# A filter stage whose block-diagonal matrix product is run in four 64x64 tiles of TensorE

## The chip, the cores and the metric

The kernel runs on one core of a Trainium2 chip. Its metric is the device time of one execution in microseconds. It was run three times: 1011.85, 1012.19 and 1015.22 us, so the median is 1012.19 us. One more execution was profiled; every duration in this text comes from that one.

Five engines matter: PE (TensorE, the matmuls, with its weight loads shown apart as PEld), DVE (VectorE), ACT (ScalarE), POOL (GpSimd) and SP, which issues most of the DMAs. Each works through its own queue in order. They wait for each other on semaphores.

## The reference, cut to what matters

Two layers alternate, twice: a global spectral filter and a token-mixing MLP, both behind a layer norm and both added to their input. The array has 2048 tokens and 640 channels.

```python
def _A_ref(x, w_r, w_i):
    X = rfft2(x)                  # over tokens and channels
    X = X * (w_r + 1j * w_i)      # 2048 x 321 complex weights
    return irfft2(X, s=(2048, 640))

x = x + _A_ref(layernorm(x), w_r, w_i)
x = x + _B_ref(layernorm(x), ...)     # gelu MLP over the tokens
x = x + _A_ref(layernorm(x), w_r, w_i)
x = x + _B_ref(layernorm(x), ...)
```

The change lies in the middle of A: the last steps of the forward transform, the multiplication by the weights, and the first step of the inverse transform.

## The kernel before, in words

All transforms are products with tables of cosines and sines. To keep nearly float32 precision, a value is split into a high and a low float16 part, and each product is done as three matmuls: high by high, high by low, low by high (`mm3`).

The token axis of 2048 is split as 16 x 128. A first step (`a0_s1`) transforms the 128 part and leaves its result in two SBUF tiles, `s1h` and `s1l`, both `[128, 80, 16, 8]`. The third axis is the group `g` (16 of them), and the last holds 8 numbers: four slots (four frequencies) with a real and an imaginary part each. The method `a1` then works group by group. It runs twice in the kernel, once per filter layer, from 59.9 to 131.7 us and from 564.7 to 634.6 us. These are the steps for a group `g`; the letters are those of the program's order lists:

- `d` (`dstage`, line 495): the channel transform, on PE. Rows of the result are 16 x 8 numbers (16 remainders of the token index by 8 slot parts), and columns are the 321 channel frequencies. There are four classes of channels. Two are cosine classes, whose sums go to PSUM bank 0 (`bk` 0 in `CL`), and two are sine classes, to bank 1. Each has 160 or 161 columns and takes four matmuls: 16 in all. In groups 0 and 1 it takes six per class.
- `ph`, `pl` (`psplit`, line 508): ACT copies the high float16 part of all 642 columns out of PSUM, DVE then makes the low part.
- `s` (`s2stage`, line 531): the transform over the 16 remainders, a 128x128 matrix on PE. For each of two outputs `ri` and two inputs `q` (bank 0 and bank 1 of `d`) there are three matmuls of 321 columns: 12 in all. The matrix mixes only numbers of the same slot.
- `ta`, `tb` (`term`, line 580): DVE multiplies the result in PSUM with the real and with the imaginary weights.
- `sa`, `sb` (`suma`, `sumb`): POOL forms the two sums of the complex product, each over 321 columns.
- `xh`, `uh` and `xl`, `ul`: the split of the product into high and low, `xh` on ACT and `xl` on POOL; `uh` and `ul` are short ACT copies of 63 columns each that repeat a part of them.
- `i` (`is2mm`, line 541): the first inverse step. It has 36 matmuls whose stationary operand has only 64 rows; the two row halves of PE (`q`) alternate.
- `Yh`, `Yl` (`yhi`, `ylo`): ACT copies the high part of the result into the tile `Y`, DVE makes the low part, in two instructions.

The order of all this is written out by hand. `group(g)` (line 647) lists the steps of a group, software-pipelined: in the time of group `g`, PE does `d` of group g+1, `i` of group g-3 and `s` of group g; DVE does `ta`, `tb` of group g-1, `pl` of g+1 and `Yl` of g-3. The loop at line 668 runs the groups 0 to 12, and the list `LAST` (line 24) holds the rest, in which group 15 is cut into two column parts. `Pin` (line 58) keeps each engine in program order. PSUM is four buffers of two banks each (`big`, line 99), taken in turn by `d`, `i` and `s`: a step can begin only when the readers of the buffer taken four steps earlier are done.

Around this, the loop also splits the first weight tile of the next layer into high and low (`wsplit`, lines 672 and 702): a quarter each after groups 8 to 11 on ACT, and in groups 9 to 12 on DVE right behind `pl`. In the first pass some small work on scales is added (`scan1`, `scale1`, `scale_b`) in groups 4 to 8.

Of the kernel before, what the change touches and what calls it, by code (L numbers as in the profile page):

```python
# [12 lines left out]
F16 = mybir.dt.float16  # L13
BF16 = mybir.dt.bfloat16
AF = mybir.ActivationFunctionType
ALU = mybir.AluOpType
# [5 lines left out]
NQ = 8  # L22
NX = 5
LAST = '''
    d14 s13 xh11 uh11 ph14 ta12 tb12 xl11 d15 pl14 s14 ul11 ta13 ph15 i10 tb13 sa12 pl15 sb12 ta14 s15 xh12 sa13 sb13
    tb14 xh13 sa14! uh13 ta15a i11 Yh10 xl12 tb15a xl13 Yl10 uh12 ul12 Yh11 sb14 sa15a s15b xh14 xl14 sb15a! ta15b
    ul13 tb15b i12 sa15b! Yh12 Yl11 uh14 xh15a ul14 i13 Yl12 i14 sb15b xl15a Yh13 xh15b uh15 Yh14 Yl13 xl15b Yl14 i15a
    ul15 Yh15a i15b Yh15b Yl15a Yl15b
# [38 lines left out]
class Layers:  # L67
# [217 lines left out]
    def a0_open(self, first=False):  # L285
        nc, A = self.nc, self.A
        p = self.pS1 = self.push("S1", side=self.sp)
        self.s1h = p.tile([128, 80, 16, 8], F16, name=f"s1h{self.n}")
        self.s1l = p.tile([128, 80, 16, 8], F16, name=f"s1l{self.n}")
        self.tD = p.tile([128, 20, 161], F16, name=f"tD{self.n}")  # L290
        self.tS2 = p.tile([128, 2, 2, 4, 128], F16, name=f"tS2{self.n}")
        self.tI2 = p.tile([128, 2, 2, 2, 128], F16, name=f"tI2{self.n}")
        p = self.pT = self.push("a0", side=self.sp)
        if first:
            self.tM = [p.tile([128, 4, 128], F32, name=f"tM{q}_{self.n}") for q in range(4)]
        else:
            self.tM = [p.tile([128, 4, 2, 128], F16, name=f"tM{q}_{self.n}") for q in range(4)]
# [56 lines left out]
    def a0_s1(self, j, fh, fl):  # L354
        ps = self.big().rearrange("p a b -> p (a b)")
        for t in range(5):
            c = slice(t * 128, t * 128 + 128)
            self.mm3(ps[:, c], (fh[:, c], fl[:, c]), (self.tM[j // 4][:, j % 4, 0], self.tM[j // 4][:, j % 4, 1]), True, True)
        return ps[:, :D].rearrange("p (a b) -> p a b", b=8)

    def a0_s1f(self, j, f):
        ps = self.big().rearrange("p a b -> p (a b)")
        for t in range(5):
            c = slice(t * 128, t * 128 + 128)
            self.PE.matmul(ps[:, c], f[:, c], self.tM[j // 4][:, j % 4], start=True, stop=True)
        return ps[:, :D].rearrange("p (a b) -> p a b", b=8)

    def a0_s1h(self, j, pv, zs=ZS):
        self.T.activation(self.s1h[:, :, j], pv, AF.Copy, scale=S1S / (zs * TS))

    def a0_s1l(self, j, pv, zs=ZS):
        self.V.scalar_tensor_tensor(
            self.s1l[:, :, j], pv, S1S / (zs * TS), self.s1h[:, :, j], op0=ALU.mult, op1=ALU.subtract
        )

    def a0_tail(self, j, z, st, pend):

        V, G, T, p = self.V, self.G, self.T, self.pT
        mv = self.stats2(p, st)
        v = self.t(p, [128, 1], F32, "v", 2)  # L380
        V.tensor_scalar(v, mv[:, 1:2], self.CA, self.CB, op0=ALU.mult, op1=ALU.add)
        m2 = self.t(p, [128, 1], F32, "nm", 2)
        V.tensor_scalar(m2, mv[:, 0:1], 2.0, None, op0=ALU.mult)
        eo = self.t(p, [128, 646], F32, "eo", 2)
        v2 = lambda a, o, w: a[:, o:o + 2 * w].rearrange("p (a b) -> p a b", a=2)[:, :, 0:160]
        za, zb = v2(z, 1, 161), v2(z, 321, 160)
        G.tensor_tensor(v2(eo, 322, 161), za, zb, op=ALU.subtract)
        r = self.t(p, [128, 1], F32, "r", 2)
        G.tensor_tensor(r, v, self.mh, op=ALU.pow)
        V.scalar_tensor_tensor(v2(eo, 1, 161), za, m2, zb, op0=ALU.subtract, op1=ALU.add)  # L390
        V.tensor_scalar(eo[:, 0:162:161], z[:, 0:162:161], mv[:, 0:1], None, op0=ALU.subtract)
        sc = S1S / (ZS * TS)
        m = self.tM[j // 4]
        eb = eo[:, 0:644].rearrange("p (a b) -> p a b", a=2)
        ea, eb = eb[:, :, 0:160], eb[:, :, 161:321]
        fs = []
        for i, (c, w) in enumerate(((slice(0, 128), 512), (slice(128, 160), 128))):
            f = self.t(p, [128, w], F32, f"ft{i}", 1)
            f4 = f.rearrange("p (c b) -> p c b", c=4)
            V.tensor_tensor(f4[:, 0::3], ea[:, :, c], eb[:, :, c], op=ALU.add)  # L400
            V.tensor_tensor(f4[:, 1:3], ea[:, :, c], eb[:, :, c], op=ALU.subtract)
            if i:
                V.tensor_copy(f[:, 95:128:32], eo[:, 160:482:321])
            fh, fl = (self.t(p, [128, w], F16, f"{a}t{i}", 1) for a in ("fh", "fl"))
            T.activation(fh, f, AF.Identity, scale=r)
            fs.append((f, fh, fl))
        ps = []
        for k, f, fh in pend:
            ps.append((k, self.a0_s1(k, *self.a0_lo(f, fh))))
            self.a0_s1h(*ps[-1])  # L410
        qs = []
        for i, (f, fh, fl) in enumerate(fs):
            V.scalar_tensor_tensor(fl, f, r, fh, op0=ALU.mult, op1=ALU.subtract)
            n = f.shape[1]
            q = self.big()[:, 0, :n]
            for o in range(0, n, 128):
                c = slice(o, o + 128)
                self.mm3(q[:, c], (fh[:, c], fl[:, c]), (m[:, j % 4, 0], m[:, j % 4, 1]), True, True)
            qs.append((q.rearrange("p (a b) -> p a b", b=8), slice(64 * i, 64 * i + n // 8)))
        for q in ps:  # L420
            self.a0_s1l(*q)
        for pv, q in qs:
            T.activation(self.s1h[:, q, j], pv, AF.Copy, scale=sc)
            V.scalar_tensor_tensor(
                self.s1l[:, q, j], pv, sc, self.s1h[:, q, j], op0=ALU.mult, op1=ALU.subtract
            )

    def s1_all(self, j, fh, fl):
# [5 lines left out]
    def a1(self, first):  # L434
# [49 lines left out]

        rest = [self.dram.tile([4, 32, NG, 128], F16, name=f"rest{i}_{self.n}") for i in range(2)]
        for q, a in zip(rest, (self.s1h, self.s1l)):
            nc.sync.dma_start(q.rearrange("c i g r -> (c i) g r"), a[:, 64:].rearrange("p g a b -> p g (a b)"))
        stack(G0)

        def wload(g):  # L490
            w = self.t(p, [128, 2, NL], F32, "w", 3)
            nc.sync.dma_start(w, A["w"][g])
            return w

        def dstage(g):
            ps = self.big()
            part = lambda t: tuple(s[:, t * 16 + g].rearrange("p a b -> p (a b)") for s in (self.s1h, self.s1l))
            for c, bk, o0, o1, k in CL:
                out, n = ps[:, bk, o0:o1], o1 - o0
                self.mm3(out, part(c), (self.tD[:, 2 * c, :n], self.tD[:, 2 * c + 1, :n]), True, False)  # L500
                if g < G0:
                    self.mm3(out, part(4), (self.tD[:, 8 + 2 * c, :n], self.tD[:, 9 + 2 * c, :n]), False, True)
                else:
                    i = g % NC
                    mm(out, stk[g - i][:k, c, i], self.tD[:k, 16 + c, :n], start=False, stop=True)
            return ps

        def psplit(ps):
# [17 lines left out]
        def twice(g, i):  # L526

            q = xs[g % NX][i]
            T.activation(q[:, :, NL:], q[:, :, 257:320], AF.Copy)

        def s2stage(g, ph, pl):
            sp = 1 if g == 0 else 0
            ps = self.big()
            for ri in range(2):
                for q in range(2):
                    a = tuple(self.tS2[:, h, sp, 2 * ri + q] for h in range(2))
                    b = (ph[:, q, :NL], pl[:, q, :NL])
                    self.mm3(ps[:, ri, :NL], a, b, q == 0, q == 1)
            return ps

        def is2mm(ps, g, lt):

# [56 lines left out]
        tt = collections.defaultdict(dict)  # L599
        part = {"": every, "a": slice(0, 256), "b": slice(256, NL)}  # L600
        ltile = {"": slice(0, 3), "a": slice(0, 2), "b": slice(2, 3)}
        dst = {}

        def do(op):
            name, g, c, dve = re.fullmatch(r"([a-zY]+)(\d+)([ab]?)(!?)", op).groups()
            g, W = int(g), V if dve else G
            pair = lambda: (tt[g][0], tt[g][1])
            if name == "d":
# [25 lines left out]
            elif name == "xl":  # L634
                xlo(g, part[c], tt[g][0][:, :, part[c]], W)
            elif name in ("uh", "ul"):
                twice(g, name == "ul")
            elif name == "i":
                pv[g, c] = self.big()
                for lt in range(3)[ltile[c]]:  # L640
# [6 lines left out]
        def group(g):  # L647
# [3 lines left out]
                return  # L651
            yield f"d{g + 1}"
            if g > 2:
                yield f"i{g - 3}"
            if g > 1:
                yield f"s{g}"
            if k > 0:
# [1 line left out]
            if k >= 0:  # L659
                yield from (f"ta{k}", f"tb{k}", f"sa{k}", f"sb{k}")  # L660
            yield from (f"ph{g + 1}", f"pl{g + 1}")
            if g > 2:
                yield from (f"Yh{g - 3}", f"Yl{g - 3}")
            if k > 0:
                yield f"ul{k - 1}"

        spare = lambda c: lambda: ps2[max(ps2)][:, 1, c:c + 1]
        for g in range(NG - 3):
# [19 lines left out]
                self.wopen(0)  # L688
            if first and g == 4:
                sb = self.scale_b(at=spare(400))  # L690
            if first and 4 <= g < 8:
                next(sb)
            if first and g in (5, 6):
                self.scan1(0, (g - 5,))
# [1078 lines left out]
def build_tables():  # L1773
# [45 lines left out]
    for sp in range(2):  # L1819
        for c8 in range(8):  # L1820
            slot, ri = c8 // 2, c8 % 2
            r_in = j16 * 8 + c8
            r_out = j16 * 4 + c8 % 4
            for half in range(2):
                m = slot * 32 + half * 16 + k2
# [21 lines left out]
                        i2[sp, 0, m[:, None], ty * 64 + r_out[None]] = pick(fr)  # L1847
                        i2[sp, 1, m[:, None], ty * 64 + r_out[None]] = pick(fi)
                for q, cc in enumerate((ap.real, aq.real, ap.imag, aq.imag)):
                    s2[sp, q, r_in[:, None], m[None]] = cc  # L1850


    d_i = np.zeros((321, 2, 322))
# [120 lines left out]
```

## Time and profile before

| | value |
|---|---|
| profiled execution | 1010.95 us, of which the span from first to last instruction is 1009.1 us |
| runs | 1011.85, 1012.19, 1015.22 us |
| granted TensorE clock | 0.981 on average; 1.00 throughout both passes of `a1` |
| PE busy | 966.7 us (96%), 8235 matmuls |
| DVE busy | 781.1 us (77%) |
| ACT busy | 577.0 us (57%) |
| POOL busy | 297.9 us (30%) |
| first `a1`, 59.88 to 131.65 us | 71.77 us: PE 67.71, DVE 63.06, ACT 48.77, POOL 48.19 busy |
| second `a1`, 564.65 to 634.58 us | 69.93 us: PE 66.29, DVE 61.05, ACT 44.98, POOL 47.71 busy |

Almost every instruction is recorded by one helper, so nearly all rows show line 59; rows are told apart by the names of their tiles. `ps` is a PSUM buffer, `tD`, `tS` and `tI` are the tables of `d`, `s` and `i`. A row such as `ps<-ph,tS 128*128 128x321` is a matmul with a 128x128 stationary operand and 321 columns streamed. The time of a single matmul is its latency, from its start to its last result; in a stream the next begins much earlier, so the spacing of starts is what a matmul costs. The same holds, in a smaller measure, for DVE and ACT.

### The profile page before, as it was taken

What the parts mean: (1) busy time and instruction counts of PE and PEld (TensorE: products, weight loads), DVE (VectorE), ACT (ScalarE), POOL (GpSimd) and SP (SyncE); (2) the same over time, 40 slices, a digit from 0 to 9 for tenths busy, and PEclk for the clock granted to TensorE, in tenths of its full rate; (3) what the DMA queues carried; (4) which work ended last, traced back from release to release, by engine and by line L of the source; (5) the groups of instructions that cost most, each with busy time, mean ns of one, the idle gap of its engine ahead of it and who ended that gap; (6) DMA issues with size and microseconds to landing.
All of it is one profiled execution on the core that took longest, in us unless ns stands there. A gap on an engine that the chain in (4) does not pass through costs nothing.

```text
span 1009.1 us, 20992 instructions
## 1 busy us (share of the span) xinstructions
PE 966.7 (96%) x8235; PEld 720.8 (71%) x8235; DVE 781.1 (77%) x1493; ACT 577.0 (57%) x890; POOL 297.9 (30%) x502
## 2 busy tenths in 40 slices
PE   4889999999999999999999799999999999999998
PEld 3778777667777777777777687776777777677776
DVE  7978978988767885666666699789965567998885
ACT  5857668687666464555543376684734454444531
POOL 6937857512222202222222278574000000000000
PEclk9599999999999999999999999999999999999999
DMA  7865356657667636464431455465544346756411
GB/s 232 278 191 164 117 171 218 223 208 259 216 210 261 240 132 225 126 199 127 126 117 55 146 176 169 131 220 190 168 167 159 136 142 240 243 170 200 146 45 53
DMA packets 67258, 176.44 MB, mean 175 GB/s; under 512 B 7996, under 2 KB 15320, under 8 KB 67160
## 3 DMA queue, kind: packets, MB, share of 16 engines
q1 hardware_dynamic: 59384, 146.92, 45.0%
q0 software_dynamic: 7776, 28.20, 7.5%
q8 instruction: 64, 1.05, 0.4%
q14 instruction: 34, 0.28, 0.1%
HBM read 127.24 MB, written 47.84 MB: 174 GB/s over the span
## 4 chain that ended last, share of the span: by engine, by line
PE 48%; DVE 22%; ACT 12%; POOL 8%; issue 6%; DMA 4%; SPq 0%; ACTq 0%; DVEq 0%; POOLq 0%
PE ps L59 48%; DVE wl L59 3%; POOL eo L59 3%; DVE f L59 3%; DMA xt<-x 2%; DVE st L59 2%; DVE xt L59 2%; ACT junk L59 2%; ACT z L59 2%; ACT wh L59 2%; POOL xt L59 2%; DVE s1l L59 1%; DVE Yl L59 1%; ACT xt L59 1%; DVE hl L59 1%
## 5 line engine op out<-in xcount | busy, mean ns | idle before, releaser
L59 PEld LDWEIGHTS <-wh 128*128 128x128 f16 x2602 | 251.4, 98 | 101.3 <-issue 3.1
L59 PEld LDWEIGHTS <-wl 128*128 128x128 f16 x1610 | 157.5, 98 | 62.2 <-issue 1.0
L59 PE MATMUL ps<-ul,wh 128*128 128x320 f16 x448 | 133.1, 299 | 0.0
L59 PE MATMUL ps<-uh,wl 128*128 128x320 f16 x448 | 133.1, 299 | 0.0
L59 PE MATMUL ps<-uh,wh 128*128 128x320 f16 x416 | 124.3, 299 | 0.0
L59 PE MATMUL ps<-hl,wh 128*128 128x320 f16 x496 | 102.3, 299 | 0.9 <-DVE hl L59 0.9
L59 PEld LDWEIGHTS <-wo 128*128 128x128 f16 x756 | 73.9, 98 | 29.4 <-DVE wo L59 0.8
L59 DVE SCALAR_TENSOR_TENSOR wl<-raw,s,wh 128x896 f16<-128x896 f32 (+2 forms) x64 | 75.1, 1177 | 22.5 <-ACT wh L59 19.6
L59 POOL TENSOR_TENSOR r<-v,mh 128x1 f32<-128x1 f32 x64 | 36.3, 567 | 162.1 <-DVE nm L59 152.6
L59 ACT ACTIVATE junk<-raw 128x896 bf16<-128x896 f32 (+1 forms) x60 | 59.5, 992 | 27.6 <-DMA raw<-w 24.4
L59 PE MATMUL ps<-tDi,Yh 128*128 128x322 f16 x320 | 71.3, 300 | 0.2
L59 ACT ACTIVATE wh<-raw,s 128x896 f16<-128x896 f32 (+2 forms) x68 | 67.1, 1010 | 6.0 <-DVE s L59 5.5
L59 DVE TENSOR_TENSOR f<-eo 128x256 f32<-128x256 f32 (+1 forms) x124 | 39.0, 368 | 40.6 <-POOL eo L59 40.1
L59 POOL TENSOR_TENSOR xt<-xt,ec 128x320 f32<-128x320 f32 x64 | 52.4, 841 | 34.0 <-DVE xt L59 33.9
L59 ACT ACTIVATE z<-xt,nb,r 128x640 f32<-128x640 f32 x31 | 28.5, 919 | 57.0 <-POOL z L59 45.2
L59 PE MATMUL ps<-ph,tS 128*128 128x321 f16 (+2 forms) x288 | 58.5, 286 | 1.3 <-DVE tb L59 1.3
L59 PE MATMUL ps<-u,wo 128*128 128x320 f16 x420 | 59.0, 299 | 0.5 <-DVE wo L59 0.5
L59 DVE BATCH_NORM_STATS2 st<-xt 128x6 f32<-128x320 f32 x126 | 55.3, 481 | 5.2 <-DMA xt<-x 4.5
L59 PE MATMUL ps<-hha,wh 128*128 128x320 f16 x288 | 58.1, 299 | 0.9 <-DVE wh L59 0.9
L59 POOL TENSOR_TENSOR eo<-z 128x320 f32<-128x320 f32 x62 | 53.3, 880 | 17.1 <-ACT z L59 15.1
L59 PE MATMUL ps<-tM,f 128*128 128x128 f32 x160 | 39.5, 426 | 19.6 <-DVE f L59 19.6
L59 PE MATMUL ps<-tDi,Yl 128*128 128x322 f16 x192 | 55.7, 299 | 1.5 <-DVE Yl L59 1.5
(251 smaller groups left out, 2375.9 us busy)
## 6 DMA issues: line engine op xcount, KB each, us to landing
xt<-x SPq DMA_DIRECT2D x79, 320.0 KB
raw<-w SPq DMA_DIRECT2D x32, 512.0 KB
w<-w SPq DMA_DIRECT2D x48, 321.0 KB
x<-xt SPq DMA_DIRECT2D x47, 320.0 KB
raw<-w SPq DMA_DIRECT2D x32, 448.0 KB
raw<-w2z SPq DMA_DIRECT2D x32, 448.0 KB
w1S<-sp POOLq DMA_DIRECT2D x20, 512.0 KB, 3.7
out<-xt SPq DMA_DIRECT2D x15, 320.0 KB
```

Of the source, the lines that this page charges most:

```text
L59: i = f(*a, **k)
```

## The change: four tiles, swapped halves, another order

1. **Layout.** `s1h` and `s1l` become `[128, 80, 2, 16, 4]`: the 8 slot parts are cut into two halves of two slots each, and the half is now the outer index. The 128 rows of `d`'s result are then 64 rows of slots 0 and 1 and 64 rows of slots 2 and 3, and the matrix of `s` becomes two blocks of 64x64. The writers of these tiles (`a0_s1h`, `a0_s1l`, `a0_tail`) address them accordingly, in runs of 4 numbers in place of 8.
2. **`d` of all groups.** For the sine classes (bank 1) every matmul is cut into two with 64 stationary columns each, and the two write each other's half of the partitions: the halves of bank 1 are swapped. Table rows of `tS2` are rotated by 64 for the inputs from bank 1 to match. A `d` step now has 8 matmuls of 128 columns and 16 of 64 (12 and 24 in groups 0 and 1).
3. **`s` of groups 3 to 12** is done in two halves, `sA` and `sB`, of 12 matmuls each with a 64x64 stationary operand. Four consecutive ones lie on four different tiles of PE: (row half, column half) 00, 01, 11, 10. The row half decides the output bank, so both row halves never write the same bank in one half step. `sB` adds to the regions which `sA` began, from the other row half; a chain of two waits (`follow`) keeps them apart: ACT's `uh` waits for the last matmul of `sA`, and the first matmul of `sB` waits for `uh`. The `s` of groups 0 to 2 and 13 to 15 stays as it was, 12 matmuls over the full array.
4. **Order of groups 3 to 12.** `i` of group g-3 is put between `sA` and `sB`; PSUM buffers are now taken in the order `d`, `s`, `i`. On ACT, `ph` comes ahead of `uh`, and `xh` moves to the end of the group before. On POOL, `xl` comes after `sa` and `sb`. On DVE, `Yl` is one group later and ahead of `pl`. `LAST` gets the `Yl` and `ul` that are left over, and one step of the scales in the first pass moves by a group.

```diff
-        self.s1h = p.tile([128, 80, 16, 8], F16, name=f"s1h{self.n}")
+        self.s1h = p.tile([128, 80, 2, 16, 4], F16, name=f"s1h{self.n}")
...
+        HALF = [slice(0, 64), slice(64, 128)]
...
             for c, bk, o0, o1, k in CL:
...
+                for i, (a, b) in enumerate(terms):
+                    for o, f in zip(HALF, HALF[::-1]) if bk else [(slice(0, 128),) * 2]:
+                        mm(ps[o, bk, o0:o1], a[:, f], b, start=i == 0, stop=i == len(terms) - 1)
...
+        def s2half(ps, x, half):
+
+            out = []
+            for k, (h, l) in enumerate(((0, 0), (0, 1), (1, 0))):
+                for R, C in ((0, 0), (0, 1), (1, 1), (1, 0)):
+                    ri, q = R ^ half, R ^ C
+                    out.append(mm(
+                        ps[HALF[C], ri, :NL], self.tS2[HALF[R], h, 0, 2 * ri + q, HALF[C]], x[l][HALF[R], q, :NL],
+                        start=half == 0 and k == 0, stop=half == 1 and k == 2,
+                    ))
+            return out[0], out[-1]
...
+                ins = twice(g, name == "ul")
+                if name == "uh" and g + 2 in half:
+                    follow(ins, half[g + 2])
+                    half[g + 2] = ins
+            elif name == "sA":
+                ps2[g] = self.big()
+                half[g] = s2half(ps2[g], pp[g], 0)[1]
+            elif name == "sB":
+                follow(s2half(ps2[g], pp.pop(g), 1)[0], half.pop(g))
...
             if g > 2:
-                yield f"i{g - 3}"
+                if g > 3:
+                    yield f"ul{g - 3}"
+                yield from (f"ph{g + 1}", f"sA{g}", f"uh{g - 2}", f"ta{k}", f"tb{k}", f"i{g - 3}", f"sB{g}")
+                yield from (f"sa{k}", f"sb{k}", f"xl{g - 2}")
+                if g > 3:
+                    yield f"Yl{g - 4}"
+                yield from (f"pl{g + 1}", f"Yh{g - 3}", f"xh{k}")
+                return
...
-            r_in = j16 * 8 + c8
+            r_in = c8 // 4 * 64 + j16 * 4 + c8 % 4
...
-                    s2[sp, q, r_in[:, None], m[None]] = cc
+                    s2[sp, q, (r_in[:, None] + 64 * q) % 128, m[None]] = cc
```

More of the change, by code (lines that the diff above doesn't have):

```diff
@@ L24 @@
 LAST = '''
-    d14 s13 xh11 uh11 ph14 ta12 tb12 xl11 d15 pl14 s14 ul11 ta13 ph15 i10 tb13 sa12 pl15 sb12 ta14 s15 xh12 sa13 sb13
+    d14 s13 ul10 ph14 uh11 ta12 tb12 xl11 d15 pl14 Yl9 s14 ul11 ta13 ph15 i10 tb13 sa12 pl15 sb12 ta14 s15 xh12 sa13 sb13
     tb14 xh13 sa14! uh13 ta15a i11 Yh10 xl12 tb15a xl13 Yl10 uh12 ul12 Yh11 sb14 sa15a s15b xh14 xl14 sb15a! ta15b
@@ L287, in a0_open @@
         p = self.pS1 = self.push("S1", side=self.sp)
-        self.s1h = p.tile([128, 80, 16, 8], F16, name=f"s1h{self.n}")
-        self.s1l = p.tile([128, 80, 16, 8], F16, name=f"s1l{self.n}")
+        self.s1h = p.tile([128, 80, 2, 16, 4], F16, name=f"s1h{self.n}")
+        self.s1l = p.tile([128, 80, 2, 16, 4], F16, name=f"s1l{self.n}")
         self.tD = p.tile([128, 20, 161], F16, name=f"tD{self.n}")
@@ L358, in a0_s1 @@
             self.mm3(ps[:, c], (fh[:, c], fl[:, c]), (self.tM[j // 4][:, j % 4, 0], self.tM[j // 4][:, j % 4, 1]), True, True)
-        return ps[:, :D].rearrange("p (a b) -> p a b", b=8)
+        return ps[:, :D].rearrange("p (a h b) -> p a h b", h=2, b=4)
     def a0_s1f(self, j, f):
@@ L365, in a0_s1f @@
             self.PE.matmul(ps[:, c], f[:, c], self.tM[j // 4][:, j % 4], start=True, stop=True)
-        return ps[:, :D].rearrange("p (a b) -> p a b", b=8)
+        return ps[:, :D].rearrange("p (a h b) -> p a h b", h=2, b=4)
     def a0_s1h(self, j, pv, zs=ZS):
-        self.T.activation(self.s1h[:, :, j], pv, AF.Copy, scale=S1S / (zs * TS))
+        self.T.activation(self.s1h[:, :, :, j], pv, AF.Copy, scale=S1S / (zs * TS))
     def a0_s1l(self, j, pv, zs=ZS):
         self.V.scalar_tensor_tensor(
-            self.s1l[:, :, j], pv, S1S / (zs * TS), self.s1h[:, :, j], op0=ALU.mult, op1=ALU.subtract
+            self.s1l[:, :, :, j], pv, S1S / (zs * TS), self.s1h[:, :, :, j], op0=ALU.mult, op1=ALU.subtract
         )
@@ L418, in a0_tail @@
                 self.mm3(q[:, c], (fh[:, c], fl[:, c]), (m[:, j % 4, 0], m[:, j % 4, 1]), True, True)
-            qs.append((q.rearrange("p (a b) -> p a b", b=8), slice(64 * i, 64 * i + n // 8)))
+            qs.append((q.rearrange("p (a h b) -> p a h b", h=2, b=4), slice(64 * i, 64 * i + n // 8)))
         for q in ps:
@@ L422, in a0_tail @@
         for pv, q in qs:
-            T.activation(self.s1h[:, q, j], pv, AF.Copy, scale=sc)
+            T.activation(self.s1h[:, q, :, j], pv, AF.Copy, scale=sc)
             V.scalar_tensor_tensor(
-                self.s1l[:, q, j], pv, sc, self.s1h[:, q, j], op0=ALU.mult, op1=ALU.subtract
+                self.s1l[:, q, :, j], pv, sc, self.s1h[:, q, :, j], op0=ALU.mult, op1=ALU.subtract
             )
@@ L486, in a1 @@
         for q, a in zip(rest, (self.s1h, self.s1l)):
-            nc.sync.dma_start(q.rearrange("c i g r -> (c i) g r"), a[:, 64:].rearrange("p g a b -> p g (a b)"))
+            nc.sync.dma_start(q.rearrange("c i g r -> (c i) g r"), a[:, 64:].rearrange("p g h a b -> p g (h a b)"))
         stack(G0)
@@ L493, in wload, with prods @@
             return w
+        HALF = [slice(0, 64), slice(64, 128)]
+        def prods(a, b):
+            return [(a[0], b[0]), (a[0], b[1]), (a[1], b[0])]
         def dstage(g):
             ps = self.big()
-            part = lambda t: tuple(s[:, t * 16 + g].rearrange("p a b -> p (a b)") for s in (self.s1h, self.s1l))
+            part = lambda t: tuple(s[:, t * 16 + g].rearrange("p h a b -> p (h a b)") for s in (self.s1h, self.s1l))
             for c, bk, o0, o1, k in CL:
-                out, n = ps[:, bk, o0:o1], o1 - o0
-                self.mm3(out, part(c), (self.tD[:, 2 * c, :n], self.tD[:, 2 * c + 1, :n]), True, False)
+                table = lambda i: (self.tD[:, i, :o1 - o0], self.tD[:, i + 1, :o1 - o0])
+                terms = prods(part(c), table(2 * c))
                 if g < G0:
-                    self.mm3(out, part(4), (self.tD[:, 8 + 2 * c, :n], self.tD[:, 9 + 2 * c, :n]), False, True)
+                    terms += prods(part(4), table(8 + 2 * c))
                 else:
-                    i = g % NC
-                    mm(out, stk[g - i][:k, c, i], self.tD[:k, 16 + c, :n], start=False, stop=True)
+                    terms.append((stk[g - g % NC][:k, c, g % NC], self.tD[:k, 16 + c, :o1 - o0]))
+                for i, (a, b) in enumerate(terms):
+                    for o, f in zip(HALF, HALF[::-1]) if bk else [(slice(0, 128),) * 2]:
+                        mm(ps[o, bk, o0:o1], a[:, f], b, start=i == 0, stop=i == len(terms) - 1)
             return ps
@@ L528, in twice @@
             q = xs[g % NX][i]
-            T.activation(q[:, :, NL:], q[:, :, 257:320], AF.Copy)
+            return T.activation(q[:, :, NL:], q[:, :, 257:320], AF.Copy)
         def s2stage(g, ph, pl):
@@ L539, in s2stage, with follow @@
             return ps
+        def s2half(ps, x, half):
[8 more added lines that the diff above has]
+            return out[0], out[-1]
+        def follow(ins, other):
+            self.tc.add_manual_dep(
+                ins.ins, other.ins.name,
+                mybir.DependencyInfo(mybir.DependencyClass.Sync, mybir.DependencyReason.DATA), reason="halves",
+            )
         def is2mm(ps, g, lt):
@@ L601, in a1 @@
         ltile = {"": slice(0, 3), "a": slice(0, 2), "b": slice(2, 3)}
-        dst = {}
+        dst, half = {}, {}
         def do(op):
-            name, g, c, dve = re.fullmatch(r"([a-zY]+)(\d+)([ab]?)(!?)", op).groups()
+            name, g, c, dve = re.fullmatch(r"([a-zABY]+)(\d+)([ab]?)(!?)", op).groups()
             g, W = int(g), V if dve else G
@@ L636, in do @@
             elif name in ("uh", "ul"):
-                twice(g, name == "ul")
+                ins = twice(g, name == "ul")
[7 more added lines that the diff above has]
+                follow(s2half(ps2[g], pp.pop(g), 1)[0], half.pop(g))
             elif name == "i":
@@ L661, in group @@
             yield from (f"ph{g + 1}", f"pl{g + 1}")
-            if g > 2:
-                yield from (f"Yh{g - 3}", f"Yl{g - 3}")
             if k > 0:
-                yield f"ul{k - 1}"
+                yield from (f"ul{k - 1}", f"xh{k}")
         spare = lambda c: lambda: ps2[max(ps2)][:, 1, c:c + 1]
@@ L690, in a1 @@
                 sb = self.scale_b(at=spare(400))
-            if first and 4 <= g < 8:
+            if first and 4 <= g < 7:
+                next(sb)
+            if first and g == 6:
                 next(sb)
```

## The prediction

> **What bounds the kernel now.** I read the page first, and from it only this: PE is busy nearly all the time, so the engine shares don't tell which work sets the end of this stage.
>
> ```profile
> span 1009.1 us, 20992 instructions
> PE 966.7 (96%) x8235; PEld 720.8 (71%) x8235; DVE 781.1 (77%) x1493; ACT 577.0 (57%) x890; POOL 297.9 (30%) x502
> ```
>
> So I cut each pass into two stretches at the first `wl` on DVE and asked for the busy times of each. Columns: length, then busy time and count of PE, PEld, DVE, ACT, POOL, the granted clock, the DMA share and GB/s.
>
> ```profile
> core 0: us, PE busy (x) PEld busy (x) DVE busy (x) ACT busy (x) POOL busy (x), PEclk, DMA share, GB/s
> 74.12:101.39 27.27, 27.07 (x436) 22.04 (x431) 23.53 (x44) 20.80 (x43) 21.06 (x24) 1.00 0.53 165
> 101.39:131.50 30.11, 27.32 (x501) 22.09 (x498) 30.04 (x49) 21.49 (x44) 24.03 (x30) 1.00 0.36 108
> 577.11:603.31 26.20, 26.20 (x433) 21.58 (x431) 22.78 (x35) 18.35 (x35) 21.01 (x24) 1.00 0.58 175
> 603.31:634.50 31.19, 28.34 (x514) 23.46 (x513) 30.76 (x51) 22.37 (x45) 23.26 (x30) 1.00 0.47 148
> ```
>
> In the first stretch of a pass (groups 3 to 9) PE never pauses, and DVE idles 27.27 - 23.53 = 3.74 us in the first pass and 26.20 - 22.78 = 3.42 us in the second. In the second stretch, to the end of the pass, DVE idles 0.07 and 0.43 us. Since the work of DVE is the same before and after, the pass can end earlier only by idle time of DVE that goes: **7.2 us for both passes is the most** that a faster PE can bring in these stretches, whatever it saves.
>
> The chain of waits of the first pass agrees: DVE and then PE stand at its end, while in the middle it runs over POOL and ACT.
>
> ```profile
> 89.00 1.47 POOL ta L59 x2
> 90.50 0.75 ACT xh L59
> 91.32 0.61 POOL xl L59
> 92.69 1.47 POOL ta L59 x2
> ...
> 127.25 4.39 DVE Yl L59 x10
> 131.69 7.40 PE ps L59 x52
> ```
>
> There POOL's sums wait behind `xl`, `xl` waits for ACT's `xh`, and `xh` for the sums: 92.69 - 89.00 = 3.69 us a group. The order of time on DVE shows its work and where it waits.
>
> ```profile
> 77.05 0.83 DVE L59 SCALAR_TENSOR_TENSOR pl<-ps,ph 128x642 f16<-128x642 f32 x1 [1.26 <-ACT ph L59]
> ...
> 80.73 0.83 DVE L59 SCALAR_TENSOR_TENSOR pl<-ps,ph 128x642 f16<-128x642 f32 x1 [0.34 <-ACT ph L59]
> 81.47 1.01 DVE L59 SCALAR_TENSOR_TENSOR Yl<-ps,Yh 128x384 f16<-128x384 f32 x2
> 82.40 0.88 DVE L59 SCALAR_TENSOR_TENSOR ta<-ps,sx,w 128x642 f32<-128x642 f32 x1
> 83.20 0.88 DVE L59 SCALAR_TENSOR_TENSOR tb<-ps,sx,w 128x642 f32<-128x642 f32 x1
> 84.42 0.83 DVE L59 SCALAR_TENSOR_TENSOR pl<-ps,ph 128x642 f16<-128x642 f32 x1 [0.34 <-ACT ph L59]
> ...
> 103.27 0.87 DVE L59 SCALAR_TENSOR_TENSOR ta<-ps,sx,w 128x642 f32<-128x642 f32 x1
> 104.06 0.87 DVE L59 SCALAR_TENSOR_TENSOR tb<-ps,sx,w 128x642 f32<-128x642 f32 x1
> 104.86 0.81 DVE L59 SCALAR_TENSOR_TENSOR pl<-ps,ph 128x642 f16<-128x642 f32 x1
> ...
> 107.40 0.87 DVE L59 SCALAR_TENSOR_TENSOR ta<-ps,sx,w 128x642 f32<-128x642 f32 x1
> ```
>
> By starts, DVE's work in a group without `wl` is `pl` 0.74, `Yl` 0.93, `ta` 0.80, `tb` 0.80 (104.06 to 104.86): **3.27 us**. With `wl` it is 107.40 - 103.27 = 4.13 us, more than PE takes, so groups 9 to 12 are DVE's. In groups 3 to 8, `pl` waits for ACT's `ph`, which stands behind `xh`.
>
> **The change part by part.** One group on PE, from the order of time:
>
> ```profile
> 101.13 0.30 PE L59 MATMUL ps<-tD,s1h 128*128 128x160 f16 x2
> ...
> 102.20 0.23 PE L59 MATMUL ps<-tD,stk 96*128 96x161 f16 x1
> 102.36 0.29 PE L59 MATMUL ps<-tI,xh 64*128 64x128 f16 x4
> ...
> 103.32 0.22 PE L59 MATMUL ps<-tI,xl 64*128 64x128 f16 x2
> 103.48 0.31 PE L59 MATMUL ps<-ph,tS 128*128 128x321 f16 x1
> ...
> 104.99 0.30 PE L59 MATMUL ps<-ph,tS 128*128 128x321 f16 x1
> 105.13 0.30 PE L59 MATMUL ps<-tD,s1h 128*128 128x160 f16 x2
> ```
>
> `d` has 16 matmuls, 15 steps from 101.13 to 102.20: 71 ns each, 1.14 us. `i` has 36, 34 steps to 103.32: 28 ns each, 1.02 us. `s` has 12, 11 steps from 103.48 to 104.99: 137 ns each, 1.65 us. Where the tile shape changes there is a gap: 102.27 to 102.36 and 103.38 to 103.48, 0.09 and 0.10 us; from `s` to `d`, the same shape, none. Sum 4.00 us, which is 105.13 - 101.13.
>
> *Concurrency of tiles.* `d` at 160 columns takes 71 ns, so 128 columns alone would take 57; `i` takes 28 a piece. Two row halves thus run side by side, loads included. No row shows column halves. Bounds: four at a time (six rounds of 137 ns, 0.41 us for each of `sA` and `sB`; the sine part of `d` unchanged at 8 x 71 ns = 0.57 us) or one after another (rival 3). I take four at a time, by the nearest row, `i`.
>
> *Weight loads.* All 24 loads of `s` and 16 of `d` now have 64 columns. Rows by shape of the loads (shapes, count, busy us, mean ns):
>
> ```profile
> L59 PEld LDWEIGHTS <-tS 128*128 128x128 f16 x432 | 36.7, 97 | 18.0 <-issue 3.2 <-DVE Yl L59 0.4 <-DVE tb L59 0.2
> L59 PEld LDWEIGHTS ps<-eh,tIM 128*128 128x128 f32 x128 | 22.9, 189 | 2.3 <-ACT eh L59 1.0
> L59 PEld LDWEIGHTS <-xh 64*128 64x128 f16 x768 | 28.8, 94 | 4.9 <-issue 1.9
> L59 PEld LDWEIGHTS ps<-eye,xq 128*16 128x16 f32 x2 | 0.1, 94 | 0.1
> ```
>
> A float16 load of 128 columns (97 ns) is barely longer than a float32 load of 16 (94), but the float32 load of 128 takes 189: (189 - 94) / 112 = 0.85 ns a column where loading is slow. From below the new loads cost nothing: a round of four leaves 34 ns for each load with its matmul, and `i` shows 28. From above they are slow and in series: 64 x 0.85 = 54 ns each. I take the lower end, because the loads of `i` for two row halves hide at 28 ns; the upper end is rival 2.
>
> The Trainium skill speaks against this choice: "TensorEngine Tiling (Array Packing)", section "Restrictions", says that column tiling turns the fast weight load off. The float16 and float32 rows above look like the two rates. By that rule the sum would be rival 2's, unless loads of different tiles overlap, which the same page's "Key Properties" claims and no run here shows.
>
> *Shape changes.* The group now goes 128x128, 128x64 (sine part of `d`), 64x64, 64x128 (`i`), 64x64 and back: five changes in place of two, at 0.10 us each 0.50. Bounds 0.05 (a load partly hidden) and 0.14 (the 54 ns of a slow load behind it).
>
> PE's group is then 0.57 + 0.57 + 0.41 + 1.02 + 0.41 + 0.50 = **3.48 us** in place of 4.00.
>
> *Order.* `xl` behind the sums takes POOL's loop apart: `xh` of the last group is made beforehand. But the new PSUM order adds a wait: `i` takes the buffer that `ta` and `tb` of the same group read, so `i` and `sB` queue behind `tb`, and the next `ta` waits for `sB`. That loop: `ta` 0.80, `tb` to its end 0.88, hand-over 0.03 (90.47 to 90.50 in the chain), `i` 1.02, change 0.10, `sB` 0.41, its last result 0.16 (0.30 less 0.14), hand-over 0.03: 3.43 us, or 3.53 if the change ahead of `i` isn't covered by the wait. I take 3.5. DVE then idles 3.5 - 3.27 = 0.23 us in each group without `wl`. The wait of `sB` for `uh` costs nothing: `i` covers it with 1.02 us against `ph` and `uh` on ACT; without that cover it would add up to 0.5.
>
> *Sum.* Of DVE's idle time the first wait of about 1.0 us (1.26 at 77.05) stays, as the `s` before it is the old one; six groups leave 1.4; ACT's scans in the first pass some 0.4. So 2.8 stays of 3.74 and 2.4 of 3.42: 1.9 us gained. Behind that, DVE has no gap to lose it in, and the two `d` of `LAST` (0.1 us more each) hide behind DVE; were DVE not full, they would cost 0.4. For `d` of groups 0 to 3 at the start of a pass I charge 0.1 a pass. Result: **1.7 us less**. The profiled execution, 1010.95 us (span 1009.1 and 1.85 around it), would become 1009.2. The median of the runs lies 1.24 above the profiled one, so I predict **1010.5 us**. The writers in runs of four numbers and the DMAs through `rest` cost nothing new: as many elements and DMAs as before, in the same places.
>
> **The rivals.** *Rival 1, more of DVE's gaps close.* If changes cost 0.05 and the first gap shrinks too, 1.3 to 1.5 us stay in each pass: 4.5 us less, 1007.7. For it: PE's group is far below the loop and POOL has room. Against it: the wait of `i` for `tb` stands in the program.
>
> *Rival 2, weight loads set PE's pace: slower than before.* In series at 54 ns, the sine part of `d` takes 16 x 0.054 = 0.87, each half of `s` 0.65, and the group 0.57 + 0.87 + 0.65 + 1.02 + 0.65 + 0.50 = 4.26. Six groups lose 0.26 each, groups 9 to 12 0.13 over DVE's 4.13, the start some 0.6: 2.7 a pass, 5.4 in all, 1017.6. It decides from about 47 ns a load on, where 40 loads eat up the 0.52 us saved. For it: the 189 ns rows. Against: those are float32.
>
> *Rival 3, column halves don't run side by side.* `s` then takes 24 x 0.137 = 3.29, `d` 0.57 + 16 x 0.071 = 1.71, the group 6.52. Ten groups lose about 2.45, the rest a little: 26 a pass, 1064. Nothing in the profile excludes it; the row halves speak against it.
>
> **How the numbers follow.** About 0.3%, 3.0 us, is what a measurement of this kernel tells from no change. The forecast (1008 to 1013.5, with the column loads of `d` alone exposed at its upper end) has 0.36, rival 1 0.34, rival 2 0.25 (0.02 of it within 3 us) and rival 3 0.05. So faster 0.34, same 0.38, slower 0.28. The range reaches to rival 1's better part, 1006.5, and past rival 2, 1019; it leaves out rival 3 and the floor of 7.2.
>
> **What would show it.** In the new trace: the starts of `sA` 137 ns apart for four matmuls (forecast) or more than 190 (rival 2) or 137 for one (rival 3); the sine part of `d` 0.57 or 0.87 us; five gaps of 0.1; `ta` of groups 4 to 8 some 3.5 us apart, waiting for PE, where they were 3.7 to 4.0 apart; `wl` groups still 4.13; DVE without gaps to the end. The forecast is wrong if DVE's idle time ahead of the first `wl` doesn't fall to about 2.6 us a pass, or if a gap opens behind it.

## The result: 0.57% slower

The changed kernel takes 1018.51 us in the median of six runs (1016.58 to 1019.28), the kernel before 1012.11 us in six runs (1009.48 to 1015.22). The ratio is 1.0057, with a 95% interval of 1.0041 to 1.0072. The profiled execution took 1016.58 us, with a span of 1014.8.

The same cut of each pass as in the prediction, from the `ta` of group 2 to the first `wl` and from there to the end of the pass, in the changed kernel (length, then busy times of PE, PEld, DVE, ACT, POOL, the granted clock, the DMA share and GB/s):

```profile
73.65:100.15 26.50, 23.92 (x568) 17.40 (x566) 23.75 (x44) 19.67 (x42) 20.88 (x25) 1.00 0.60 176
100.15:134.50 34.35, 26.87 (x587) 20.47 (x580) 34.28 (x51) 21.46 (x45) 22.89 (x30) 1.00 0.32 97
580.57:605.42 24.85, 24.46 (x581) 17.92 (x580) 22.58 (x34) 17.78 (x35) 20.43 (x25) 1.00 0.64 189
605.42:639.80 34.38, 27.03 (x588) 20.48 (x581) 34.31 (x51) 21.47 (x45) 22.89 (x30) 1.00 0.43 133
```

The first stretches are shorter, 26.50 and 24.85 us against 27.27 and 26.20: 2.1 us gained. The second ones are longer, 34.35 and 34.38 against 30.11 and 31.19: 7.4 us lost. The cuts end at slightly different points; measured to the end of the last `Yl`, the second stretches take 34.55 and 34.57 us against 30.63 and 31.27, 7.2 us more. In them DVE is busy throughout, and its work was meant to be the same. Grouped by shape, one group of DVE differs: the split of the weights. First the row of the kernel before, then that of the changed one.

```profile
L59 DVE SCALAR_TENSOR_TENSOR wl<-raw,s,wh 128x512 f16<-128x512 f32 x8 | 7.9, 991 | 0.0
```

```profile
L59 DVE SCALAR_TENSOR_TENSOR wl<-raw,s,wh 128x512 f16<-128x512 f32 x8 | 15.5, 1942 | 0.0
```

The same eight instructions take 15.5 us in place of 7.9, 1.94 us each in place of 0.99. That is 7.6 us, as much as the second stretches lose; 0.4 us of DVE's idle time in the second pass went the other way. Put in order of time, DVE and then POOL of the changed kernel show why:

```profile
102.01 0.88 DVE L59 SCALAR_TENSOR_TENSOR ta<-ps,sx,w 128x642 f32<-128x642 f32 x1
102.81 0.87 DVE L59 SCALAR_TENSOR_TENSOR tb<-ps,sx,w 128x642 f32<-128x642 f32 x1
103.60 1.01 DVE L59 SCALAR_TENSOR_TENSOR Yl<-ps,Yh 128x384 f16<-128x384 f32 x2
104.53 0.82 DVE L59 SCALAR_TENSOR_TENSOR pl<-ps,ph 128x642 f16<-128x642 f32 x1
105.26 1.94 DVE L59 SCALAR_TENSOR_TENSOR wl<-raw,s,wh 128x512 f16<-128x512 f32 x1
107.13 0.88 DVE L59 SCALAR_TENSOR_TENSOR ta<-ps,sx,w 128x642 f32<-128x642 f32 x1
```

```profile
103.83 0.76 POOL L59 TENSOR_TENSOR ta<-ta,tb 128x321 f32<-128x321 f32 x1 [2.28 <-DVE tb L59]
104.54 0.75 POOL L59 TENSOR_TENSOR ta<-tb,ta 128x321 f32<-128x321 f32 x1
105.24 1.42 POOL L59 TENSOR_TENSOR xl<-ta,xh 128x642 f16<-128x642 f32 x1
```

`xl` on POOL begins at 105.24 and ends at 106.66. `wl` begins at 105.26 and ends at 107.20, 0.54 us after `xl`. Unhindered it takes 0.74 us (the row at 607.82 below), so it got through a small part of its work at most while `xl` ran. A group with `wl` takes 107.13 - 102.01 = 5.12 us, not 4.13. In the kernel before, `wl` fell beside the short sums, and the collision was there in small:

```profile
101.11 0.75 POOL L59 TENSOR_TENSOR ta<-ta,tb 128x321 f32<-128x321 f32 x1
101.82 1.20 POOL L59 TENSOR_TENSOR ta<-tb,ta 128x321 f32<-128x321 f32 x1
```

```profile
101.39 1.03 DVE L59 SCALAR_TENSOR_TENSOR wl<-raw,s,wh 128x512 f16<-128x512 f32 x1
...
607.82 0.74 DVE L59 SCALAR_TENSOR_TENSOR wl<-raw,s,wh 128x512 f16<-128x512 f32 x1
```

There `wl` ran until 102.42, and the second sum, which takes 0.75 us alone, took 1.20 and ended 0.60 after it. The eight `wl` of the kernel before range from 0.74 to 1.34 us; the one at 607.82 began only 0.18 us before the end of a first sum and ahead of the second one, and it was the second sum that took longer, 1.22 us.

PE itself did what was forecast. A group of the changed kernel:

```profile
92.06 0.31 PE L59 MATMUL ps<-tD,s1h 128*128 128x160 f16 x2
...
92.57 0.23 PE L59 MATMUL ps<-tD,stk 98*128 98x161 f16 x1
92.74 0.33 PE L59 MATMUL ps<-tD,s1h 128*64 128x160 f16 x4
...
93.26 0.24 PE L59 MATMUL ps<-tD,stk 96*64 96x161 f16 x2
93.43 0.33 PE L59 MATMUL ps<-ph,tS 64*64 64x321 f16 x4
93.59 0.31 PE L59 MATMUL ps<-pl,tS 64*64 64x321 f16 x4
93.73 0.31 PE L59 MATMUL ps<-ph,tS 64*64 64x321 f16 x4
93.99 0.28 PE L59 MATMUL ps<-tI,xh 64*128 64x128 f16 x4
```

Four 64x64 matmuls of 321 columns begin 0.14 to 0.16 us after the four before: the four tiles run side by side. The sine part of `d` takes from 92.74 to 93.33, as long as the cosine part before it. Each change of shape costs 0.09 to 0.12 us.

### The profile page after: what moved, and what is told of

It reads as the page before. It is cut to its first block, busy times and chain, and to the rows that moved or that the text cites. A ratio compares the mean times of both kernels' runs of the same rounds, so it can differ in the third digit from the quotient of the medians.

```text
span 1014.8 us, 22035 instructions
## 1 busy us (share of the span) xinstructions
PE 962.5 (95%) x8747; PEld 707.6 (70%) x8747; DVE 788.7 (78%) x1493; ACT 574.6 (57%) x890; POOL 295.7 (29%) x502
## 5 line engine op out<-in xcount | busy, mean ns | idle before, releaser
L59 DVE SCALAR_TENSOR_TENSOR wl<-raw,s,wh 128x896 f16<-128x896 f32 (+2 forms) x64 | 82.7, 1296 | 22.7 <-ACT wh L59 19.8
L59 PE MATMUL ps<-hha,wl 128*128 128x320 f16 x256 | 53.4, 299 | 0.0
```

The costliest lines, as they stand in the source:

```text
L59: i = f(*a, **k)
```

## The experiments

Theory A: the whole loss is `wl` standing still beside `xl`, brought about by the new order, and the tiles are a small gain. Rival B: the tiles cost the time, by shape changes, loads, or the clock at the start of the second pass, and `wl` is a side effect. Runs are compared with runs of the kernel before on the same chip (median 1011.4 us for the first four, 1011.78 for the others).

**e1: `xl` ahead of the sums.**

```diff
-                yield from (f"sa{k}", f"sb{k}", f"xl{g - 2}")
+                yield from (f"xl{g - 2}", f"sa{k}", f"sb{k}")
```

> The changed kernel with one step moved: in groups 3 to 12, POOL does xl of group g-2 ahead of sa and sb, not behind them, so that it falls beside ta and tb on DVE and POOL is free when DVE makes wl. Theory A (the loss is wl on DVE standing still while POOL runs xl: 1.94 us in the changed kernel, 0.99 before, 8 times): wl falls to 0.75 to 1.0 us, the groups with wl take 4.0 to 4.2 us in place of 5.11, some 8 us less than the changed kernel, ratio to the kernel before 0.996 to 1.000. Rival B (the loss is the tiles themselves: shape changes, more loads, or the slower clock at the start of the second pass): no shorter, ratio 1.004 to 1.007.

Measured: 1012.02 us, ratio 1.0005 (0.9990 to 1.0019). DVE in groups with `wl`:

```profile
107.22 0.74 DVE L59 SCALAR_TENSOR_TENSOR wl<-raw,s,wh 128x512 f16<-128x512 f32 x1
107.88 0.88 DVE L59 SCALAR_TENSOR_TENSOR ta<-ps,sx,w 128x642 f32<-128x642 f32 x1
111.13 0.74 DVE L59 SCALAR_TENSOR_TENSOR wl<-raw,s,wh 128x512 f16<-128x512 f32 x1
111.79 0.88 DVE L59 SCALAR_TENSOR_TENSOR ta<-ps,sx,w 128x642 f32<-128x642 f32 x1
```

Seven of the eight `wl` take 0.73 to 0.74 us (one takes 1.28), and the group 111.79 - 107.88 = 3.91. The loss is gone with the tiles still there, so rival B falls. The ratio lies just above the range expected, whose upper end its interval includes. POOL's old loop is back ahead of `wl`: `xl` waits for ACT's `xh`, which waits for the sums, and the groups there are 96.38 - 92.69 = 3.69 us apart. That this is all that is missing is not shown.

```profile
92.69 1.42 POOL L59 TENSOR_TENSOR xl<-ta,xh 128x642 f16<-128x642 f32 x1 [0.85 <-ACT xh L59]
...
96.38 1.43 POOL L59 TENSOR_TENSOR xl<-ta,xh 128x642 f16<-128x642 f32 x1 [0.85 <-ACT xh L59]
```

The same `xl` shows which instructions are not affected: `tb` on DVE, with one input in PSUM, runs beside it from 92.65 on and takes its usual 0.88 us, and `xl` its usual 1.42.

**e2: `wl` between `ta` and `tb`.**

```diff
-                if op == "pl%d" % (g + 1) and 9 <= g < 13:
+                if op == "ta%d" % (g - 1) and 9 <= g < 13:
```

> The changed kernel with wl moved on DVE from behind pl to between ta and tb, where POOL has come to the end of xl and waits for tb. Theory A: wl meets only the last 0.4 us of xl and takes some 1.1 to 1.2 us; the groups with wl take about 4.4 us in place of 5.11, some 5 us less than the changed kernel, ratio 0.999 to 1.003. Rival B: ratio 1.004 to 1.007 as in the changed kernel.

Measured: 1016.6 us, ratio 1.0051 (1.0031 to 1.0071). A miss in time, and by the time alone rival B (1.004 to 1.007) would fit; the trace shows that `wl` isn't slowed:

```profile
102.17 0.89 DVE L59 SCALAR_TENSOR_TENSOR ta<-ps,sx,w 128x642 f32<-128x642 f32 x1 [0.23 <-POOL ta L59]
103.64 0.75 DVE L59 SCALAR_TENSOR_TENSOR wl<-raw,s,wh 128x512 f16<-128x512 f32 x1 [0.58 <-ACT wh L59]
107.08 0.89 DVE L59 SCALAR_TENSOR_TENSOR ta<-ps,sx,w 128x642 f32<-128x642 f32 x1 [0.23 <-POOL ta L59]
```

`wl` takes 0.75 us, but it waits 0.58 for its high part from ACT, and both lie inside the loop in which PE's `i` waits for `tb`: 4.91 us a group. This explains the time, and no further run tested it. A place free of POOL is not enough; what is queued behind `wl` counts too.

**e3: the old kernel with `wl` between `ta` and `tb`**, the same edit in the kernel before.

> The kernel before, with nothing of the change, but wl on DVE moved to between ta and tb, where POOL is about to run xl. Theory A: wl takes 1.8 to 1.95 us there too, 0.9 more, 8 times, in a stretch that DVE sets: 6 to 7 us slower than the kernel before, ratio 1.005 to 1.007, with full 128x128 products throughout. Rival B: wl's place doesn't matter, ratio 0.999 to 1.001.

Measured: 1014.3 us, ratio 1.0030 (1.0013 to 1.0046): slower, but by about half of what was expected. The two passes differ. DVE in the first and in the second pass, then POOL:

```profile
105.17 0.74 DVE L59 SCALAR_TENSOR_TENSOR wl<-raw,s,wh 128x512 f16<-128x512 f32 x1
```

```profile
607.25 1.97 DVE L59 SCALAR_TENSOR_TENSOR wl<-raw,s,wh 128x512 f16<-128x512 f32 x1
```

```profile
105.55 1.65 POOL L59 TENSOR_TENSOR xl<-ta,xh 128x642 f16<-128x642 f32 x1 [0.85 <-ACT xh L59]
```

```profile
607.26 1.42 POOL L59 TENSOR_TENSOR xl<-ta,xh 128x642 f16<-128x642 f32 x1 [0.85 <-ACT xh L59]
```

In the first pass `wl` begins 0.38 us ahead of `xl`; it runs in 0.74, and POOL pays, 1.65 in place of 1.42. In the second, both begin within 0.01 us, POOL goes first, and `wl` takes 1.97. The groups take 3.92 us in the first pass and 5.15 in the second, which is why only half of the loss came. This kernel has nothing of the change in it. So the two instructions exclude each other but for 0.1 to 0.2 us, and the one that comes first runs at full speed.

The Trainium skill states this rule: "SBUF — State Buffer", section "Who interferes with whom", says that a DVE instruction with two SBUF inputs contends with a GpSimd instruction that reads SBUF, and that the order of issue decides who blocks. `wl` reads `raw` and `wh` from SBUF, and the traces agree, with 1.94 and 1.97 us against 0.74.

**e4: the full-array `s` in the new order.**

```diff
             elif name == "sA":
-                ps2[g] = self.big()
-                half[g] = s2half(ps2[g], pp[g], 0)[1]
+                ps2[g] = s2stage(g, *pp.pop(g))
             elif name == "sB":
-                follow(s2half(ps2[g], pp.pop(g), 1)[0], half.pop(g))
+                pass
```

> The changed kernel with the s of groups 3 to 12 as 12 matmuls over the full array again (the halves of the sine part of d stay swapped), in the new order. Theory A: the loss stays and the small gain ahead of wl goes: PE's group is 0.57 + 0.57 + 1.65 + 1.02 and four shape changes of 0.1, 4.2 us, in place of 3.57, wl still 1.9: 1 to 5 us slower than the changed kernel, ratio 1.006 to 1.011. Rival B: the loss goes with the tiles, ratio 0.999 to 1.002.

Measured: 1023.5 us, ratio 1.0123 (1.0100 to 1.0146). Without the tiles of `s` the changed kernel is another 5.0 us slower than with them: as large as theory A allowed, and by the ratio just above its 1.006 to 1.011. Most groups ahead of `wl` in the second pass are 4.23 us apart, as expected, and `wl` is still long:

```profile
L59 DVE SCALAR_TENSOR_TENSOR wl<-raw,s,wh 128x512 f16<-128x512 f32 x8 | 14.0, 1748 | 0.0
```

The loss needs the new order and not the tiles of `s`. The split of `d` is still in this run.

**e5: `wl` right behind `tb`.**

```diff
-                if op == "pl%d" % (g + 1) and 9 <= g < 13:
+                if op == "tb%d" % (g - 1) and 9 <= g < 13:
```

> The changed kernel with wl on DVE moved from behind pl to right behind tb, in groups 9 to 12. There POOL has nothing to do until tb is done, so wl and sa begin at nearly the same moment. Theory A, with what the earlier runs added (whoever of DVE's wl and POOL begins first runs alone, the other stands still until it ends): if wl begins first, wl takes 0.74 and sa waits, the groups with wl take 3.95 us in place of 5.11: 9 us less than the changed kernel, ratio to the kernel before 0.997 to 0.999. If sa begins first, wl waits 0.75 or 1.5 us for it, 1.3 to 2.2 us, and the groups take 4.5 to 5.4: ratio 1.001 to 1.008. Rival B (the tiles cost the time): 1.004 to 1.007 whatever wl does.

Measured: 1009.66 us, ratio 0.9976 (0.9959 to 0.9992), as expected for the case in which `wl` comes first. DVE, then POOL:

```profile
102.69 0.88 DVE L59 SCALAR_TENSOR_TENSOR tb<-ps,sx,w 128x642 f32<-128x642 f32 x1
103.48 0.74 DVE L59 SCALAR_TENSOR_TENSOR wl<-raw,s,wh 128x512 f16<-128x512 f32 x1
104.14 1.02 DVE L59 SCALAR_TENSOR_TENSOR Yl<-ps,Yh 128x384 f16<-128x384 f32 x2
...
106.60 0.88 DVE L59 SCALAR_TENSOR_TENSOR tb<-ps,sx,w 128x642 f32<-128x642 f32 x1
```

```profile
103.71 1.13 POOL L59 TENSOR_TENSOR ta<-ta,tb 128x321 f32<-128x321 f32 x1 [0.70 <-DVE tb L59]
```

DVE begins `wl` before `tb`'s result has reached POOL, so POOL waits: `sa` takes 1.13 in place of 0.75, on an engine with room. A group takes 106.60 - 102.69 = 3.91 us.

**e6 and e7: `wl` out of the groups**, done behind the last `Yl` of the pass, in the changed kernel (e6) and in the kernel before (e7). The edit is the same:

```diff
-                if op == "pl%d" % (g + 1) and 9 <= g < 13:
-                    self.wsplit(0, quarter(g - 9)[0], hi=False, part=quarter(g - 9)[1])
...
         for op in LAST.split():
             do(op)
+        for q in range(4):
+            self.wsplit(0, quarter(q)[0], hi=False, part=quarter(q)[1])
```

> The changed kernel with the four wl of each pass taken out of the groups and done right behind the last Yl of the pass, where DVE waited 2.6 us for ACT's eh in both profiles. Nothing is left out. Theory A: all groups run at 3.57 us; against the kernel with wl moved in the same way and nothing else (the run after this), 1 to 2.5 us less, since the loss came from wl alone; against the kernel before, ratio 0.992 to 0.996. Rival B: as slow or slower than the run after this by 3 us or more, ratio above 0.999.

> The kernel before, nothing of the change, with the four wl of each pass done right behind the last Yl of the pass. If DVE sets the end of the pass, as the prediction has it, the pass ends earlier by at most the 4 us that wl took of DVE, and by less where PE's 4.0 us a group takes over: 2 to 5 us less than the kernel before, ratio 0.995 to 0.998. If PE had set it, 0.999 to 1.001.

Measured: e6 1008.3 us, ratio 0.9960 (0.9946 to 0.9974), the fastest of all; e7 1010.86 us, ratio 0.9988 (0.9976 to 1.0000). Layout, tiles and order are worth 1010.86 - 1008.3 = 2.6 us once `wl` is out of the way; each of the two ratios is known to within about 1.3 us. In e6 the groups with `wl` before are now 3.57 us apart, as expected. e7 gained less than expected: without `wl`, the old groups are still 3.7 us apart in the first pass, the length of POOL's loop, and 4.0 in the second, the length of PE's work, so taking work from DVE brings little there. In e6 the four `wl` of a pass stand where DVE waited for ACT before:

```profile
129.63 2.72 DVE L59 SCALAR_TENSOR_TENSOR wl<-raw,s,wh 128x512 f16<-128x512 f32 x4
132.33 0.89 DVE L59 SCALAR_TENSOR_TENSOR el<-ps,cxe,eh 128x644 fp32r<-128x644 f32 x1
```

**e8: the tiles in the old order** of POOL, ACT and DVE; PE keeps its new one. The list `LAST` and the steps of the groups ahead of group 3 are adapted to it.

```diff
...
-                if g > 3:
-                    yield f"ul{g - 3}"
-                yield from (f"ph{g + 1}", f"sA{g}", f"uh{g - 2}", f"ta{k}", f"tb{k}", f"i{g - 3}", f"sB{g}")
-                yield from (f"sa{k}", f"sb{k}", f"xl{g - 2}")
-                if g > 3:
-                    yield f"Yl{g - 4}"
-                yield from (f"pl{g + 1}", f"Yh{g - 3}", f"xh{k}")
+                yield from (f"xh{k - 1}", f"sA{g}", f"uh{k - 1}", f"ta{k}", f"tb{k}", f"i{g - 3}", f"sB{g}")
+                yield from (f"xl{k - 1}", f"sa{k}", f"sb{k}", f"ph{g + 1}", f"pl{g + 1}")
+                yield from (f"Yh{g - 3}", f"Yl{g - 3}", f"ul{k - 1}")
...
```

> The changed kernel with its layout, split d and four tiles, but with the old order of POOL, ACT and DVE in groups 3 to 12 as far as it can be had (xh, uh, xl of group g-2 ahead of the sums, then ph, pl, wl, Yh, Yl, ul; PE keeps d, sA, i, sB). Theory A: wl runs beside the sums again, 0.9 to 1.05 us; POOL's loop over xh sets the other groups at 3.7 to 3.9 us: ratio 0.997 to 1.001. Rival B: the tiles still cost what they cost, ratio 1.004 to 1.007.

Measured: 1011.22 us, ratio 0.9999 (0.9985 to 1.0013), and `wl` is back at its old length:

```profile
L59 DVE SCALAR_TENSOR_TENSOR wl<-raw,s,wh 128x512 f16<-128x512 f32 x8 | 7.8, 977 | 0.0
```

Tiles without the new order bring nothing: the groups ahead of `wl` are mostly 3.7 us apart again, which fits POOL's loop over `xh` in the chain of waits, and those with `wl` 4.13. The new order without the tiles of `s` (e4) loses 12 us. Only both together, with `wl` out of POOL's way (e5 and e6), gain.

## Why the prediction was wrong, point by point

- **The step that failed** is in the reading of DVE: "Since the work of DVE is the same before and after", with "With `wl` it is 107.40 - 103.27 = 4.13 us, more than PE takes, so groups 9 to 12 are DVE's", carried into the sum as "Behind that, DVE has no gap to lose it in". It took the length of a DVE instruction as fixed while the change moved what runs on POOL beside it. Those groups took 5.12 us: eight `wl` at 1.94 instead of 0.99, 7.6 us. "`xl` behind the sums takes POOL's loop apart" was right, and it was this move that put `xl` beside `wl`. The sign was in the trace of before: the second sum 1.20 us beside `wl` and 0.75 elsewhere, and `wl` itself between 0.74 and 1.34.
- **What stays of DVE's idle time** was forecast as 2.8 and 2.4 us. The windows show 26.50 - 23.75 = 2.75 and 24.85 - 22.58 = 2.27, and the gain of 2.1 us ahead of the first `wl` compares with the 1.9 forecast. That the sums agree so closely is partly luck: the first wait, put at 1.0 us, was 0.92 and 0.61, and one later group a pass waited another 0.72 and 0.55 us for ACT's `ph`, which the forecast didn't have. Gain and loss together, 7.2 - 2.1 = 5.1 us, compare with 5.7 between the two profiled spans and 5.8 by the ratio.
- **Concurrency, loads, shape changes**: as taken. The new loads show 105 ns (64x64) and 112 (128x64), against 97 for 128x128, and hide at 35 to 40 ns for a load with its matmul. Whether they are of the slow kind that rival 2 feared doesn't show; if they are, they overlap:

```profile
L59 PEld LDWEIGHTS <-tS 64*64 64x64 f16 x480 | 10.5, 105 | 6.9 <-ACT xh L59 2.0
L59 PEld LDWEIGHTS <-s1h 128*64 128x64 f16 x288 | 12.3, 112 | 4.4 <-issue 0.3
```

- **The start of a pass** was mis-sized: charged with 0.1 us for `d` of groups 0 to 3, it costs 0.5 in the second pass. There it takes 13.0 us from the last `s1l` (the low part of the step ahead of `d`) to the `ta` of group 2 in e1, e5 and e8, and 12.5 in the kernel before and in e3; in all five the clock was up by then (the last section shows one in which it wasn't).
- **The loop of DVE and PE** was put at 3.5 us; in the second pass of the changed kernel most groups ahead of `wl` run at 3.57 (`ta` at 595.02 and 598.59). The rows name POOL as the one waited for, but its sum was done at 594.74, and the last matmuls of `sB` only at 594.60 + 0.31 = 594.91:

```profile
593.99 0.75 POOL L59 TENSOR_TENSOR ta<-tb,ta 128x321 f32<-128x321 f32 x1
594.60 0.31 PE L59 MATMUL ps<-ph,tS 64*64 64x321 f16 x4
595.02 0.89 DVE L59 SCALAR_TENSOR_TENSOR ta<-ps,sx,w 128x642 f32<-128x642 f32 x1 [0.23 <-POOL ta L59]
598.59 0.89 DVE L59 SCALAR_TENSOR_TENSOR ta<-ps,sx,w 128x642 f32<-128x642 f32 x1 [0.23 <-POOL ta L59]
```

- **Rival 2** gave 1017.6 us and comes close to the time, but not by its mechanism: the loads hide, and e5 and e6 are faster than the kernel before with all of them in place. **Rival 3** is excluded by the 0.14 us between rounds of four. **Rival 1** needed the wait of `i` for `tb` to go, and it is there: between 74 and 134 us the weight loads of `i` wait 8.2 us for `tb`.

## What to carry to other kernels

Before an instruction is moved in time, look at what then runs beside it on DVE and POOL: an instruction of DVE with both inputs in SBUF and one of POOL shut each other out here (`wl` against `xl` and the sums), and the one that begins second carries the whole wait in its own length, which the profile counts as busy. Compare the lengths of the same instruction in different surroundings in the trace of before; 1.20 against 0.75 us was the warning. In these runs such work did best where POOL was about to wait anyway (e5), or where DVE itself waited and nothing due soon stood behind it (e6).

## What the runs showed of the hardware that was not expected

A blocked instruction isn't idle in the profile: in the second stretches DVE of the changed kernel shows 34.28 of 34.35 us busy, while its four `wl` stood still for 1.94 - 0.74 = 1.20 us each, 4.8 us.

The clock at the start of the second pass differs between executions, whichever the kernel. The changed kernel, then the kernel before, then e7, which has nothing of the change, at the start of the pass (the column behind POOL is the granted clock):

```profile
566.00:568.00 2.00, 1.72 (x12) 1.31 (x12) 0.84 (x2) 0.09 (x1) 0.00 (x0) 0.50 0.56 223
```

```profile
566.00:568.00 2.00, 2.00 (x31) 2.00 (x29) 0.32 (x1) 0.44 (x1) 0.00 (x0) 1.00 1.04 391
```

```profile
566.00:568.00 2.00, 2.00 (x18) 2.00 (x16) 0.77 (x2) 0.88 (x2) 0.00 (x0) 0.50 0.67 224
```

So the lower clock is no mark of the tiles. It blurs profiles by about two microseconds: from the last `s1l` to the `ta` of group 2, e7 took 14.89 us and the kernel before 12.48.

Why POOL goes first when the two begin 0.01 or 0.02 us apart (e3, second pass, and the changed kernel) was not tried.
